# A windowed-attention stage whose values are loaded by head on partition halves, with half of the keys on ScalarE's DMA queue

## The chip, the cores and the metric

The kernel runs on one core of a Trainium2 chip. The metric is device time in microseconds (us) of one execution. The kernel before was timed in three runs: 833.41, 840.51 and 843.72 us, median 840.51 us. The changed kernel is timed in the same way. One execution of the kernel before was also recorded by the hardware profiler, and all rows of a trace below come from that one.

## What is computed

Three layers follow each other. The first is attention with eight heads over 4 sequences of 576 tokens, 64 numbers per head. Four heads see the last 32 tokens, the other four see every fourth of the last 128. The second layer sends each token to one of eight experts, the third is a dense layer.

```python
# q, k, v: (4, 8, 576, 64) float32
scores = matmul(q, k^T) / sqrt(64)
mask_plain = (rel >= 0) & (rel < 32)                    # heads 0..3
mask_dil   = (rel >= 0) & (rel < 128) & (rel % 4 == 0)  # heads 4..7
attn = softmax(where(mask, scores, -1e9));  x = matmul(attn, v)  # -> (2304, 512)
# experts: each token goes to the best of 8 by cosine similarity
out[mask] = gate_w * (relu(x[mask] @ w1[e]) @ w2[e])    # 512 -> 1024 -> 512
# dense: 512 -> 2048 -> 512
h = x @ w_in;  out = (h * cos(h)) @ w_out
```

## The kernel before

The 2304 tokens are 18 tiles of 128. Inputs come in pairs of tiles: nine pairs, each with a queries tile `q`, keys and values. Two heads share the 128 partitions, 64 each: partitions 0 to 63 hold one head (j = 0), 64 to 127 the other (j = 1), and four such head pairs (`pr`) make the eight heads.

**Keys and values.** `kr` is a ring of six tiles of keys, `[128, 2, 6, 512]`, block-diagonal: half j of the partitions holds head j's keys in plane j, and zeros in the other plane, so that one matmul over 128 partitions gives the scores of both heads side by side. `vb` is built in the same way: two buffers `[128, 2, 2, 4, 4, 65]`, one pair of tiles each, half j filled in plane j and the rest set to zero once by GpSimd (L349, L352, L368). The 65th column is one, so a product also gives the row sum. Because a half and a plane go together, keys and values are loaded by two DMAs of 64 partitions each (L333 for keys, 256 KB each; L338 for values, 520 KB each). Queries come in one DMA over 128 partitions (L330, 512 KB). All of these are issued by SyncE (SP), in program order.

**A tile.** `emit_S` (L425, L429) adds the mask by one bf16 matmul and the scores by 16 float32 matmuls of 32 columns of weights. VectorE (DVE) takes the maximum and subtracts it, ScalarE (ACT) takes the exponential (`emit_E`, L445), TensorE (PE) transposes (L452), ACT copies the transpose to `pT` (L457), and `emit_PV` (L465) multiplies it by the values: 16 matmuls over 128 partitions with 130 columns, into two PSUM banks by `pr // 2`. `emit_N` divides by the row sum. Later in the pipeline come the transposes of x (L487), the logits of the experts, and the store of x, 256 KB a tile, to the DRAM tensor `x_d`, issued by ACT (L525).

**What sets the order.** The first 15 tiles run in a hand-written loop (`TURN` = 15), whose steps stand in one string, `ORDER`, with lags of 0 to 3 tiles: scores of tile i, products of tile i - 1, logits of tile i - 3. Its step `l`, in the middle of an iteration between the copy `pT` and the exponential on ACT, is the place where the next loads are issued: in odd iterations keys and queries of pair i // 2 + 2, in even ones from 2 on the values of pair i // 2 + 1. The last three tiles, the ranking of tokens by expert and the preparation of the first expert weights (loads `wst`, 1024 KB each, L241, whose absolute sums ACT takes at L250) are ordered by a planner from due times. In its terms the values of pair p may be loaded after the products of tile 2p - 3. At 154 us SP loads the list of tokens by expert (`ix`, L856); expert matmuls begin at 171 us, the dense layer at about 450 us.

**DMA semaphores.** DMAs issued by SP and by ACT's queue take eight semaphores in turn (DMAHW0 to DMAHW7). A DMA that takes a semaphore waits at its queue until the DMA that had that semaphore before has landed.

Of the kernel before, what the change touches and what calls it, by code (L numbers as in the profile page):

```python
# [11 lines left out]
F32 = mybir.dt.float32  # L12
# [7 lines left out]
ALU = mybir.AluOpType  # L20
# [145 lines left out]
def tile_kernel(ctx, tc, qh, kh, vh, c16_h, c32_h, emb, tau, w1h, w2h, win_h, wout_h, out):  # L166
    nc = tc.nc
    V, S, G, T, SP = nc.vector, nc.scalar, nc.gpsimd, nc.tensor, nc.sync
# [59 lines left out]
    with tc.manual_schedule():  # L228
        wst = ctx.enter_context(tc.tile_pool(name="wst", bufs=5, side="left"))
        with ExitStack() as p12:  # L230
# [5 lines left out]
            plan = Plan(HOLD1, BIAS1)  # L236
# [69 lines left out]
            with ExitStack() as p1:  # L306
                krp = p1.enter_context(tc.tile_pool(name="krp", bufs=1, side="right"))
                cst = p1.enter_context(tc.tile_pool(name="p1c", bufs=1, side="right"))
# [7 lines left out]
                sm = p1.enter_context(tc.tile_pool(name="sm", bufs=3, side="right"))  # L316
                ps_s = p1.enter_context(tc.tile_pool(name="ps_s", bufs=2, space=PSUM))
                ps_1 = p1.enter_context(tc.tile_pool(name="ps_1", bufs=1, space=PSUM))
                kr = krp.tile([128, 2, RING, 512], F32, name="kr")
                krb = kr.rearrange("p j s (b i) -> p j (s b) i", i=32)  # L320
                vb = [cst.tile([128, 2, 2, 4, 4, 65], F32, name=f"vb{i}") for i in range(2)]
                blank = cst.tile([128, E * REG // 64], U32, name="blank")
                tau_b = cst.tile([128, 1], F32, name="tau_b")
                ent = cst.tile([128, 4, E], F32, name="ent")
# [2 lines left out]
                def load(p, i0=0, i1=2):  # L327
                    if i0 == 0:
                        q_t[p] = qp.tile([128, 2, 4, 128], F32, name="q", tag="q")
                    SP.dma_start(out=q_t[p][:, i0:i1], in_=qh[p, :, i0:i1])  # L330
                    s0 = (2 * p) % RING
                    for j in range(2):
                        SP.dma_start(out=kr[64 * j:64 * j + 64, j, s0 + i0:s0 + i1], in_=kh[p, 64 * j:64 * j + 64, i0:i1])  # L333

                def load_v(p, i0=0, i1=2):
                    v = vb[p % 2]
                    for j in range(2):
                        SP.dma_start(out=v[64 * j:64 * j + 64, j, i0:i1], in_=vh[p, 64 * j:64 * j + 64, i0:i1])  # L338


                zc = cst.tile([128, 1], F32, name="zc")
# [4 lines left out]
                other = lambda j: slice(64 * j, 64 * j + 64)  # L346
                for j in range(2):
                    S.activation(out=kr[other(j), 1 - j, 0], in_=zc[other(j)].to_broadcast([64, 512]), func=ACTF.Copy)
                    G.memset(vb[0][other(j), 1 - j, 0], 0.0)  # L349
                for j in range(2):  # L350
                    V.memset(kr[other(j), 1 - j, 1:RING - 1], 0.0)
                    G.memset(vb[0][other(j), 1 - j, 1], 0.0)  # L352
                c16_load = lambda a, b: SP.dma_start(out=c16[:, a:b], in_=c16_h[:, a:b])
                load(0, 0, 1)
                c16_load(0, 640)
                load(0, 1, 2)
# [7 lines left out]
                load_v(0, 1, 2)  # L364
                c16_load(1152, 3 * 128 + NT * 128)
                load_v(1)
                for j in range(2):
                    G.memset(vb[1][other(j), 1 - j], 0.0)  # L368
                G.memset(zero, 0)
                G.memset(blank, 0)  # L370
                SP.dma_start(out=tok_r.rearrange("(p a) w -> p (a w)", p=128), in_=blank)
# [9 lines left out]
                def set_up(k):  # L381
                    if k == 0:
                        V.tensor_copy(out=pay[:, :, 0], in_=tokf)
                        V.tensor_scalar(out=base, in0=iota, scalar1=float(REG), scalar2=None, op0=ALU.mult)
                        V.tensor_copy(out=base0, in_=base)
                        V.tensor_tensor(out=tri, in0=iota.unsqueeze(1).to_broadcast([128, E, E]), in1=iota.unsqueeze(2).to_broadcast([128, E, E]), op=ALU.is_lt)
                        V.tensor_tensor_reduce(out=esq, in0=emb_t, in1=emb_t, scale=1.0, scalar=0.0, op0=ALU.mult, op1=ALU.add, accum_out=ess)
                    elif k == 1:
                        G.tensor_tensor(out=ess, in0=ess, in1=half[0:E, 0:1], op=ALU.pow)
                    elif k == 2:  # L390
                        V.tensor_scalar(out=ess, in0=ess, scalar1=1e-6, scalar2=None, op0=ALU.add)
                        V.reciprocal(out=ess, in_=ess)
                        V.reciprocal(out=tau_b, in_=tau_b)
                        V.tensor_scalar(out=emb_t, in0=emb_t, scalar1=ess, scalar2=tau_b[0:E], op0=ALU.mult, op1=ALU.mult)
                    elif k == 3:
                        for c in range(4):
                            T.transpose(eps[:, c, :], emb_t[:, c * 128:(c + 1) * 128], ident[0:E, 0:E])
                    else:
                        V.tensor_copy(out=ent, in_=eps)

                st = {}
# [56 lines left out]
                    st["pT", t] = pT  # L458

                def emit_PV(t):  # L460
                    pT, v = st.pop(("pT", t)), vb[(t // 2) % 2][:, :, t % 2]
                    xps = ps_1.tile([128, 2, 512], F32, name="xps", tag="xps")
                    for pr in (2, 3, 0, 1):
                        for u in range(4):
                            T.matmul(out=xps[32 * u:32 * u + 32, pr // 2, 130 * (pr % 2):130 * (pr % 2) + 130],  # L465
                                     lhsT=pT[:, pr, 32 * u:32 * u + 32], rhs=v[:, :, u, pr, :], start=True, stop=True)
                    st["xps", t] = xps

                def emit_N(t, k):
                    xv = st["xps", t][:, :, 0:260].rearrange("p a (h c) -> p a h c", c=65)  # L470
                    if k == 0:
                        st["rs", t] = sm.tile([128, 2, 4, 1], F32, name="rs", tag="rs")
                        V.tensor_scalar(out=st["rs", t], in0=xv[:, :, :, 64:65], scalar1=1e-9, scalar2=None, op0=ALU.add)
                    elif k == 1:
                        V.reciprocal(out=st["rs", t], in_=st["rs", t])
                    elif k == 2:
                        xd = st["xd", t] = xp.tile([128, 256], F32, name="xd", tag="xd", bufs=2)
                        V.tensor_tensor(out=xd.rearrange("p (h c) -> p h c", c=64), in0=xv[:, 1, :, 0:64], in1=st["rs", t][:, 1].to_broadcast([128, 4, 64]), op=ALU.mult)
                    else:
                        x = st["x", t] = xp.tile([128, D], F32, name="x", tag="x")  # L480
                        V.tensor_tensor(out=x[:, 0:256].rearrange("p (h c) -> p h c", c=64), in0=xv[:, 0, :, 0:64], in1=st["rs", t][:, 0].to_broadcast([128, 4, 64]), op=ALU.mult)

                def emit_XT(t):
                    x, xd = st["x", t], st.pop(("xd", t))
# [145 lines left out]
                def fetch(what, p):  # L630
                    if p < NT // 2 and (what, p) not in fetched:
                        fetched.add((what, p))
                        (load if what == "k" else load_v)(p)
# [8 lines left out]
                for i in range(TURN):  # L642
                    if 0 < i < 4:
                        for k in ((0, 1), (2,), (3, 4))[i - 1]:
                            set_up(k)
                    count = {}
                    for what in ORDER.split():
                        if what == "r":
                            pump()
                        elif what == "w":  # L650
                            if i >= W_FROM:
                                take(early)
                        elif what == "L":
                            for _ in range(WLOADS.count(i)):
                                take(loads)
                        elif what == "l":
                            if i % 2 == 1:
                                fetch("k", i // 2 + 2)
                            elif i > 1:
                                fetch("v", i // 2 + 1)  # L660
                        else:
                            lag, *parts = tile_jobs[what]
                            if i >= lag:
                                parts[count.get(what, 0)](i - lag)
                            count[what] = count.get(what, 0) + 1
# [3 lines left out]
                for q in plan.free:  # L669
                    plan.free[q] = 0.0  # L670
                for p in range(2, NT // 2):
                    for what, after in (("k", "S"), ("v", "PV")):
                        if (what, p) not in fetched:
                            plan.add((what, p), "DMA", 2.9, lambda what=what, p=p: fetch(what, p), (after, 2 * p - 3))
                        else:
                            plan.at((what, p), 0.0)
                for t in range(TURN - 3, NT):
# [158 lines left out]
            with ExitStack() as p2:  # L836
# [42 lines left out]
                ixs, xrs, xps = {}, {}, {}  # L879
# [158 lines left out]
                for e in range(E):  # L1038
                    plan.add(("list", e), "DMA", 0.5, lambda e=e: x_do(e, 0, "list"), ("sent", NT - 1), *[("gate", e - 2, c) for c in range(3)])
                    for c in range(3):  # L1040
                        k = 3 * e + c
# [13 lines left out]
                    for f in range(8):  # L1055
                        pe(("mm", 2 * e, f), 1.35, lambda e=e, f=f: h_part(e, f), ("x lo", e, 0), ("x lo", e, 1), ("lo", 2 * e, f * CUT // 8), *([("h lo", (4 * e + f // 2 - 3) // 4, (4 * e + f // 2 - 3) % 4)] if f % 2 == 0 else []))
                        if f % 2:
                            k = f // 2
# [7 lines left out]
                    for i, ds in enumerate(halves):  # L1066
                        for f in range(8):
                            name = ("mm", 2 * e + 1, f) if not i else ("mm", 2 * E, f)
# [73 lines left out]
        with ExitStack() as p3:  # L1142
# [124 lines left out]
            for b, (t0, n) in enumerate(blocks):  # L1267
# [11 lines left out]
                for t in range(n // 128):  # L1279
# [11 lines left out]
                    c = t0 // 128 + t  # L1291
# [66 lines left out]
```

## Time and profile before

| what | value |
|---|---|
| median of three runs | 840.51 us |
| the profiled execution | 842.5 us |
| its span in the trace | 840.7 us |
| TensorE busy | 749.1 us, 89% of the span |
| ScalarE, VectorE, GpSimd busy | 448.9, 438.6, 188.8 us |
| mean granted TensorE clock | 0.935 of full speed |

The span runs from the first to the last instruction of the trace; the execution's own time is 1.8 us longer. TensorE is the busiest engine over the whole span, but the share is uneven: the attention stage, the first fifth of the span, is where it waits most, and it is the only stage that the change touches.

### The profile page before, as it was taken

Reading aid. Unit: us, or ns where it says so; the run is one execution under the profiler, and the core shown is the slowest. Engines: PE = TensorE matmul, PEld = TensorE weight load, DVE = VectorE, ACT = ScalarE, POOL = GpSimd, SP = SyncE. Lnnn points to the kernel's source line nnn. Section 1 sums busy time; section 2 is a strip of 40 time slices with the busy share of each in tenths; the row PEclk is TensorE's granted clock in tenths of the full one; section 3 lists DMA queues with packets and bytes.
Section 4 is the critical chain, followed back from the end, with each engine's and each line's share of the span. In section 5 each row is a group of like instructions: output and inputs, shape, how many; then the busy total and the mean of one; then the engine's idle time right before and its main releaser. Section 6 shows DMA issues by size and latency. Waiting matters only on the chain. (4 is left out here: it accounts for less than half of the span.)

```text
span 840.7 us, 14816 instructions
## 1 busy us (share of the span) xinstructions
PE 749.1 (89%) x5961; PEld 492.2 (59%) x5961; DVE 438.6 (52%) x893; ACT 448.9 (53%) x705; POOL 188.8 (22%) x230
## 2 busy tenths in 40 slices
PE   6897779494999889988997989999999999999995
PEld 3676667273898768876883434444444445645642
DVE  5354525655678587857797983154105511531510
ACT  2343536362778698857566992177117701832820
POOL 4021203375010010100000440234103411421420
PEclk8888968887899989998999999999999999999999
DMA  8979881559855566635321000100000000000000
GB/s 220 257 170 253 219 294 52 212 102 103 262 177 194 192 218 211 241 126 165 115 76 55 1 0 1 46 5 2 26 26 1 0 26 26 1 14 26 1 13 26
DMA packets 27444, 87.32 MB, mean 104 GB/s; under 512 B 9688, under 2 KB 10200, under 8 KB 22240
## 3 DMA queue, kind: packets, MB, share of 16 engines
q1 hardware_dynamic: 20256, 70.42, 28.8%
q0 software_dynamic: 4512, 11.04, 4.7%
q10 hardware_dynamic: 2592, 4.72, 1.8%
q8 instruction: 55, 0.90, 0.5%
q14 instruction: 29, 0.24, 0.1%
HBM read 76.53 MB, written 9.64 MB: 102 GB/s over the span
## 5 line engine op out<-in xcount | busy, mean ns | idle before, releaser
L1188 PE MATMUL u<-yb,win 128*128 128x512 f16 (+1 forms) x924 | 179.8, 357 | 0.0
L1226 PEld LDWEIGHTS <-g 128*128 128x128 f16 x864 | 85.0, 98 | 105.7 <-issue 4.2
L1226 PE MATMUL o<-wst,g 128*128 128x512 f16 x672 | 145.7, 379 | 0.0
L1188 PEld LDWEIGHTS <-win 128*128 128x128 f16 x924 | 90.4, 98 | 88.8
L1004 PE MATMUL hps<-xT,wt 128*128 128x256 f16 x768 | 98.2, 292 | 19.9 <-DVE xT L877 13.9
L1222 POOL TENSOR_TENSOR g<-gg,g 128x512 f16<-128x512 f32 (+1 forms) x80 | 85.4, 1071 | 125.3 <-ACT g L1220 124.2
L973 PE MATMUL y<-h,wt 128*128 128x256 f16 (+1 forms) x1152 | 107.7, 255 | 1.1 <-DVE h L963 0.3
L973 PEld LDWEIGHTS <-wt 128*128 128x128 f16 x1152 | 96.4, 98 | 11.2 <-issue 2.2
L1004 PEld LDWEIGHTS <-wt 128*128 128x128 f16 x768 | 80.3, 105 | 35.5 <-issue 19.6
L1217 DVE SCALAR_TENSOR_TENSOR gg<-u,q 128x512 f32<-128x512 f32 (+1 forms) x80 | 50.6, 637 | 73.7 <-ACT q L1214 73.5
L1209 ACT ACTIVATE kk<-u,quart,ku 128x512 int32<-128x512 f32 (+1 forms) x80 | 58.1, 732 | 51.3 <-PE u L1188 51.1
L275 DVE SCALAR_TENSOR_TENSOR wt<-wst,wsc,wt 128x1024 f16<-128x1024 f32 x64 | 79.4, 1280 | 3.8 <-ACT wt L273 2.8
L273 ACT ACTIVATE wt<-wst,wsc 128x1024 f16<-128x1024 f32 x64 | 69.0, 1142 | 12.3 <-DVE wsc L217 7.9
L250 ACT ACTIVATE junk<-wst 128x2048 bf16<-128x2048 f32 x32 | 61.0, 1906 | 24.7 <-DMA wst<-in_w1h 24.6
L861 POOL DMA_INDIRECT xr<-x_d,ix x24 | 28.0, 1166 | 203.4 <-PE hps L870 103.0
L1212 DVE SCALAR_TENSOR_TENSOR q<-u,ku,kk 128x512 f32<-128x512 f32 (+1 forms) x80 | 54.8, 689 | 32.3 <-ACT kk L1209 32.3
L1214 ACT ACTIVATE q<-q,quart 128x512 f32<-128x512 f32 (+1 forms) x80 | 53.1, 669 | 5.7 <-DVE q L1212 5.4
L1288 ACT ACTIVATE osb<-o,ku 128x512 f32<-128x512 f32 x6 | 4.1, 687 | 97.3 <-PE o L1226 97.3
L1290 DVE TENSOR_SCALAR osb<-o,ku 128x512 f32<-128x512 f32 x8 | 6.0, 751 | 92.4 <-PE o L1226 92.4
L1294 POOL DMA_INDIRECT out<-osb,idx x18 | 17.5, 971 | 150.0 <-DVE osb L1290 93.7
L1220 ACT ACTIVATE g<-gg 128x512 f16<-128x512 f32 (+1 forms) x80 | 45.8, 575 | 1.4 <-DVE gg L1217 1.4
L1226 PE MATMUL u<-wst,g 128*128 128x512 f16 x192 | 43.4, 390 | 2.7 <-ACT wst L808 2.1
(197 smaller groups left out, 889.0 us busy)
## 6 DMA issues: line engine op xcount, KB each, us to landing
wst<-in_w1h SPq DMA_DIRECT2D x16, 1024.0 KB, 6.6
wst<-in_w2h SPq DMA_DIRECT2D x16, 1024.0 KB, 5.1
vb<-in_vh SPq DMA_DIRECT2D x16, 520.0 KB, 9.4
raw<-in_winh SPq DMA_DIRECT2D x16, 512.0 KB, 7.2
raw<-in_wouth SPq DMA_DIRECT2D x16, 512.0 KB, 3.9
x_d<-x ACTq DMA_DIRECT2D x18, 256.0 KB, 5.2
q<-in_qh SPq DMA_DIRECT2D x8, 512.0 KB, 8.3
kr<-in_kh SPq DMA_DIRECT2D x16, 256.0 KB, 9.7
```

The costliest lines, as they stand in the source:

```text
L250: S.activation(out=junk[:, 0:k], in_=src, func=ACTF.Square, accum_out=wmx[m][:, i:i + 1])
L273: S.activation(out=hi, in_=src, func=ACTF.Copy, scale=wsc[:, m, 0:1])
L275: V.scalar_tensor_tensor(out=lo, in0=src, scalar=wsc[:, m, 0:1], in1=hi, op0=ALU.mult, op1=ALU.subtract)
L973: T.matmul(out=dst(d), lhsT=w[:, a, 128 * d:128 * d + 128], rhs=src(f, b), start=f == 0 and k == 0 and d in firsts, stop=f == 7 and k == 2 ...
L1004: T.matmul(out=hps[e, f // 2][:, f % 2], lhsT=w[:, a, 128 * c:128 * c + 128], rhs=xts[e][0][:, 4 * b + c, :], start=n == 0, stop=n == 11)
L1188: T.matmul(out=us[f], lhsT=win[f][:, a, 128 * c:128 * c + 128], rhs=ybs[b][:, a2, c, :], start=k == 0, stop=k == 11)
L1209: S.activation(out=ks[f], in_=us[f], func=ACTF.Identity, scale=ku[:, 0:1], bias=quart[:, 0:1])
L1212: V.scalar_tensor_tensor(out=qs[f], in0=us[f], scalar=ku[:, 0:1], in1=ks[f], op0=ALU.mult, op1=ALU.subtract)
L1214: S.activation(out=qs[f], in_=qs[f], func=ACTF.Sin, scale=PI2, bias=quart[:, 1:2])
L1217: V.scalar_tensor_tensor(out=gs[f], in0=us[f], scalar=SH, in1=qs[f], op0=ALU.mult, op1=ALU.mult)
L1222: G.tensor_tensor(out=g_t[f][:, 1], in0=gs[f], in1=g_t[f][:, 0], op=ALU.subtract)
L1226: T.matmul(out=o, lhsT=g_t[f][:, a, 128 * t:128 * t + 128], rhs=wout[f][:, a2, :], start=f == 0 and k == 0, stop=f == 15 and k == 2)
```

## The change

Values. `vb` becomes three buffers `[128, 2, 4, 4, 65]` without the second plane: half j of the partitions holds head j's values and there are no zeros. One DMA over 128 partitions loads a pair (1040 KB), and GpSimd's memsets are gone. In the loop the values are fetched one pair earlier; in the planner they wait for the products of tile 2p - 5.

Products. Each of the 16 matmuls over 128 partitions and 130 columns becomes two, one for each head, over 64 partitions and 65 columns. The two write to different PSUM banks (j instead of `pr // 2`). `emit_N` reads the same number of elements in another arrangement.

Keys. The half j = 0 stays on SP's queue, the half j = 1 is issued by ACT.

```diff
-                vb = [cst.tile([128, 2, 2, 4, 4, 65], F32, name=f"vb{i}") for i in range(2)]
+                vb = [cst.tile([128, 2, 4, 4, 65], F32, name=f"vb{i}") for i in range(3)]
+                head = lambda j: slice(64 * j, 64 * j + 64)
-                    for j in range(2):
-                        SP.dma_start(out=kr[64 * j:64 * j + 64, j, s0 + i0:s0 + i1], in_=kh[p, 64 * j:64 * j + 64, i0:i1])
+                    for j, queue in enumerate((SP, S)):
+                        queue.dma_start(out=kr[64 * j:64 * j + 64, j, s0 + i0:s0 + i1], in_=kh[p, 64 * j:64 * j + 64, i0:i1])
                 def load_v(p, i0=0, i1=2):
-                    v = vb[p % 2]
-                    for j in range(2):
-                        SP.dma_start(out=v[64 * j:64 * j + 64, j, i0:i1], in_=vh[p, 64 * j:64 * j + 64, i0:i1])
+                    SP.dma_start(out=vb[p % 3][:, i0:i1], in_=vh[p, :, i0:i1])
-                    G.memset(vb[0][other(j), 1 - j, 0], 0.0)
-                    G.memset(vb[0][other(j), 1 - j, 1], 0.0)
-                for j in range(2):
-                    G.memset(vb[1][other(j), 1 - j], 0.0)
                 def emit_PV(t):
-                            T.matmul(out=xps[32 * u:32 * u + 32, pr // 2, 130 * (pr % 2):130 * (pr % 2) + 130],
-                                     lhsT=pT[:, pr, 32 * u:32 * u + 32], rhs=v[:, :, u, pr, :], start=True, stop=True)
+                            for j in range(2):
+                                T.matmul(out=xps[32 * u:32 * u + 32, j, 65 * pr:65 * pr + 65], lhsT=pT[head(j), pr, 32 * u:32 * u + 32],
+                                         rhs=v[head(j), u, pr, :], start=True, stop=True)
                 def emit_N(t, k):
-                    xv = st["xps", t][:, :, 0:260].rearrange("p a (h c) -> p a h c", c=65)
+                    xv = st["xps", t][:, :, 0:260].rearrange("p j (r c) -> p r j c", c=65)
-                            elif i > 1:
-                                fetch("v", i // 2 + 1)
+                            else:
+                                fetch("v", i // 2 + 2)
-                    for what, after in (("k", "S"), ("v", "PV")):
+                    for what, after in (("k", ("S", 2 * p - 3)), ("v", ("PV", 2 * p - 5))):
```

On SP's queue, from the values of pair 1 on, the program of before reads as follows (`vb_131` and `vb_132` are the two buffers, `x2` the two halves).

```order
L338 DMA vb_132<-in_vh 64x2080 x2
L371 DMA tok_r<-blank 128x336
L330 DMA q<-in_qh 128x1024
L333 DMA kr<-in_kh 64x1024 x2
L338 DMA vb_131<-in_vh 64x2080 x2
L330 DMA q<-in_qh 128x1024
L333 DMA kr<-in_kh 64x1024 x2
```

In the changed kernel the same place of SP's queue reads as below, with a third buffer `vb_133`.

```order
L338 DMA vb_132<-in_vh 128x2080
L367 DMA tok_r<-blank 128x336
L338 DMA vb_133<-in_vh 128x2080
L332 DMA q<-in_qh 128x1024
L335 DMA kr<-in_kh 64x1024
L338 DMA vb_131<-in_vh 128x2080
L332 DMA q<-in_qh 128x1024
L335 DMA kr<-in_kh 64x1024
```

The values of pair 2 now stand ahead of the queries and keys of pair 2, and so on for each pair: values are one pair ahead, and a pair takes three DMAs of SP's queue instead of five.

ACT's program in the changed kernel starts as follows, up to iteration 3 of the loop (`DMAHW` names the DMA semaphore that a transfer waits for, `zc` is a column of zeros); in the kernel before the rows at L335 are not there.

```order
L348 ACT_TABLE_LOAD
L348 ACTIVATE kr<-zc 64x512 [waits DVE_49]
L348 ACTIVATE kr<-zc 64x512
L335 DMA kr<-in_kh 64x512 x2
L335 DMA kr<-in_kh 64x1024 [waits DMAHW1_49]
L441 ACTIVATE pt<-sb 128x512 [waits DVE_49]
L453 ACTIVATE pT<-ptp 128x512 [waits PE_49]
L335 DMA kr<-in_kh 64x1024 [waits DMAHW6_49]
...
L453 ACTIVATE pT<-ptp 128x512 [waits PE_49,Activation_49]
L335 DMA kr<-in_kh 64x1024 [waits DMAHW5_49,DMAHW4_49]
L441 ACTIVATE pt<-sb 128x512 [waits DVE_49]
```

ACT issues three halves before its first exponential, and from then on one in each odd iteration, between a copy `pT` and the next exponential. The semaphores that these rows wait for were taken by transfers issued two or three iterations earlier.

On PE a stretch of the loop's start reads as follows in the changed kernel. In the kernel before it is the same, but the row of the products is `xps<-vb_131,pT 32x130 x16`.

```order
L421 LDWEIGHTS c_111
L421 MATMUL s<-c_111 128x512
L425 MATMUL s<-kr,q 32x128 x16
L448 MATMUL ptp<-c_63,pt 128x128 x4
L462 MATMUL xps<-vb_131,pT 32x65 x32
```

There are twice as many products with half the columns each; the order of PE's work around them has not moved.

## Rows read from the trace of the kernel before

**Rows 1.** The page: span, and TensorE and DMA busy tenths in 40 slices.
```profile
span 840.7 us, 14816 instructions
...
PE   6897779494999889988997989999999999999995
...
DMA  8979881559855566635321000100000000000000
```

**Rows 2.** Windows: stretch and length, busy us by engine, granted clock, DMA share, GB/s.
```profile
28.00:32.00 4.00, 2.48 (x45) 1.99 (x43) 1.67 (x4) 1.42 (x4) 0.00 (x0) 1.00 1.02 228
63.00:66.00 3.00, 3.00 (x58) 2.46 (x50) 2.20 (x11) 1.13 (x3) 0.00 (x0) 1.00 0.93 374
112.00:118.00 6.00, 3.40 (x58) 2.55 (x60) 1.49 (x6) 3.61 (x6) 0.00 (x0) 0.78 1.01 418
```

**Rows 3.** DMA issues on the page: count, KB each, median us to landing.
```profile
vb<-in_vh SPq DMA_DIRECT2D x16, 520.0 KB, 9.4
x_d<-x ACTq DMA_DIRECT2D x18, 256.0 KB, 5.2
q<-in_qh SPq DMA_DIRECT2D x8, 512.0 KB, 8.3
kr<-in_kh SPq DMA_DIRECT2D x16, 256.0 KB, 9.7
```

**Rows 4.** Windows of the attention stage, columns as in rows 2.
```profile
0.00:100.00 100.00, 82.30 (x1236) 61.16 (x1240) 50.51 (x172) 40.12 (x86) 22.59 (x35) 0.86 0.89 220
0.00:114.40 114.40, 90.34 (x1365) 67.58 (x1365) 55.76 (x192) 43.51 (x93) 22.59 (x35) 0.85 0.90 232
116.50:133.50 17.00, 16.57 (x151) 14.50 (x155) 5.28 (x26) 9.94 (x19) 4.24 (x7) 0.50 0.43 168
```

**Rows 5.** PE's timeline: start us, us, engine, line, [idle before, releaser].
```profile
17.26 0.58 PE L425 MATMUL s<-c 128*128 128x512 bf16 x1 [3.90 <-DMA c<-in_c]
...
51.45 0.38 PE L425 MATMUL s<-c 128*128 128x512 bf16 x1
...
54.43 1.09 PE L465 MATMUL xps<-vb,pT 128*32 128x130 f32 x32
...
55.95 0.38 PE L425 MATMUL s<-c 128*128 128x512 bf16 x1
...
71.18 1.10 PE L429 MATMUL s<-kr,q 128*32 128x128 f32 x32 [4.27 <-DMA kr<-in_kh]
...
99.75 1.08 PE L429 MATMUL s<-kr,q 128*32 128x128 f32 x32
...
107.45 1.94 PE L429 MATMUL s<-kr,q 128*32 128x128 f32 x32 [6.29 <-DMA kr<-in_kh]
...
170.92 0.37 PE L1004 MATMUL hps<-xT,wt 128*128 128x256 f16 x1 [0.47 <-ACT xT L875]
```

**Rows 6.** Waits of SP's DMA queue, 0 to 160 us: us in total, times, longest.
```profile
SPq L333 <- DMA x_d<-x: 23.3, 4, 9.6
SPq L338 <- DMA x_d<-x: 11.0, 2, 10.4
SPq L338 <- PE xps L465: 10.8, 3, 6.5
SPq L241 <- DMA x_d<-x: 8.9, 2, 4.5
```

**Rows 7.** ACT's timeline: the first activations, and a wait for weights.
```profile
2.02 1.26 ACT L348 ACTIVATE kr<-zc 64x512 f32<-64x512 f32 x2
...
114.39 1.91 ACT L250 ACTIVATE junk<-wst 128x2048 bf16<-128x2048 f32 x1 [10.58 <-DMA wst<-in_w1h]
```

**Rows 8.** SP's timeline: the first keys, and the list of tokens by expert.
```profile
1.19 1.19 SPq L333 DMA_DIRECT2D kr<-in_kh  x2
...
154.22 0.38 SPq L856 DMA_DIRECT2D ix<-tok_r  x1
```

**Rows 9.** Groups by shape, 0 to 130 us: GpSimd's memset of a buffer of values.
```profile
L368 POOL MEMSET vb<- 64x2080 f32 x2 | 3.7, 1828 | 0.1
```

**Rows 10.** Windows of the expert stage and of the dense stage, columns as in rows 2.
```profile
170.00:450.00 280.00, 242.81 (x2436) 213.22 (x2435) 202.95 (x345) 197.07 (x270) 42.40 (x53) 0.93 0.56 166
450.00:800.00 350.00, 346.01 (x1690) 165.96 (x1689) 145.25 (x231) 174.35 (x288) 98.62 (x106) 0.99 0.03 12
```

More of the change, by code (lines that the diff above doesn't have):

```diff
@@ L460, in emit_PV @@
                 def emit_PV(t):
-                    pT, v = st.pop(("pT", t)), vb[(t // 2) % 2][:, :, t % 2]
+                    pT, v = st.pop(("pT", t)), vb[(t // 2) % 3][:, t % 2]
                     xps = ps_1.tile([128, 2, 512], F32, name="xps", tag="xps")
@@ L464, in emit_PV @@
                         for u in range(4):
-                            T.matmul(out=xps[32 * u:32 * u + 32, pr // 2, 130 * (pr % 2):130 * (pr % 2) + 130],
-                                     lhsT=pT[:, pr, 32 * u:32 * u + 32], rhs=v[:, :, u, pr, :], start=True, stop=True)
+                            for j in range(2):
+                                T.matmul(out=xps[32 * u:32 * u + 32, j, 65 * pr:65 * pr + 65], lhsT=pT[head(j), pr, 32 * u:32 * u + 32],
+                                         rhs=v[head(j), u, pr, :], start=True, stop=True)
                     st["xps", t] = xps
                 def emit_N(t, k):
-                    xv = st["xps", t][:, :, 0:260].rearrange("p a (h c) -> p a h c", c=65)
+                    xv = st["xps", t][:, :, 0:260].rearrange("p j (r c) -> p r j c", c=65)
                     if k == 0:
-                        st["rs", t] = sm.tile([128, 2, 4, 1], F32, name="rs", tag="rs")
+                        st["rs", t] = sm.tile([128, 4, 2, 1], F32, name="rs", tag="rs")
                         V.tensor_scalar(out=st["rs", t], in0=xv[:, :, :, 64:65], scalar1=1e-9, scalar2=None, op0=ALU.add)
@@ L477, in emit_N @@
                         xd = st["xd", t] = xp.tile([128, 256], F32, name="xd", tag="xd", bufs=2)
-                        V.tensor_tensor(out=xd.rearrange("p (h c) -> p h c", c=64), in0=xv[:, 1, :, 0:64], in1=st["rs", t][:, 1].to_broadcast([128, 4, 64]), op=ALU.mult)
+                        V.tensor_tensor(out=xd.rearrange("p (r j c) -> p r j c", r=2, j=2), in0=xv[:, 2:4, :, 0:64], in1=st["rs", t][:, 2:4].to_broadcast([128, 2, 2, 64]), op=ALU.mult)
                     else:
                         x = st["x", t] = xp.tile([128, D], F32, name="x", tag="x")
-                        V.tensor_tensor(out=x[:, 0:256].rearrange("p (h c) -> p h c", c=64), in0=xv[:, 0, :, 0:64], in1=st["rs", t][:, 0].to_broadcast([128, 4, 64]), op=ALU.mult)
+                        V.tensor_tensor(out=x[:, 0:256].rearrange("p (r j c) -> p r j c", r=2, j=2), in0=xv[:, 0:2, :, 0:64], in1=st["rs", t][:, 0:2].to_broadcast([128, 2, 2, 64]), op=ALU.mult)
                 def emit_XT(t):
@@ L671, in tile_kernel @@
                 for p in range(2, NT // 2):
-                    for what, after in (("k", "S"), ("v", "PV")):
+                    for what, after in (("k", ("S", 2 * p - 3)), ("v", ("PV", 2 * p - 5))):
                         if (what, p) not in fetched:
-                            plan.add((what, p), "DMA", 2.9, lambda what=what, p=p: fetch(what, p), (after, 2 * p - 3))
+                            plan.add((what, p), "DMA", 2.9, lambda what=what, p=p: fetch(what, p), after)
                         else:
```

## The prediction

> **What bounds the kernel now.** I read the page first: TensorE (PE) is at nine tenths or more from the 25th of the 40 slices to the last but one, and lowest in the first eight, of which the first six (21 us each) have the DMA engines at seven tenths or more [rows 1]. The change touches only these first 154 us. The later stages take over whatever is gained there: in the dense stage PE is busy 346.0 of 350 us, and in the expert stage 242.8 of 280 us with DMA at 0.56, so neither waits for transfers that an earlier start would make later [rows 10]. A microsecond gained when expert matmuls begin (170.92 us [rows 5]) is a microsecond at the end.
>
> In the attention stage the reader should see two near-equal limits. PE alone needs 4.50 us a tile at full clock: the mask matmuls of two tiles start at 51.45 and 55.95 us with no stall between [rows 5]. Yet from the masks at 17.26 us (tile 2) to the scores at 99.75 us (tile 15) 13 tiles take 82.5 us, 6.3 each. The long stalls of PE name keys: 4.27 us at 71.18, 6.29 us at 107.45 [rows 5]. The DMA engines are busy 0.89 of the first 100 us, at only 220 GB/s [rows 4]. Two things waste them. Transfers to 64 partitions are slow: with values and keys alone in flight the engines are full at 228 GB/s, against 374 with queries and weights and 418 with weights [rows 2]. And SP's queue stands still: 23.3 us in four waits of keys for a store of x, 11.0 us in values for the same, 10.8 us in values for products that still read the buffer [rows 6].
>
> **The change part by part.**
>
> *Values in one load.* A pair of tiles is 2 x 520 KB [rows 3], 1.065 MB. At 228 GB/s it takes 4.67 us of the DMA engines, at 380 (between 374 and 418) 2.80 us: 1.87 us less per pair. By 99.75 us eight pairs were loaded (15.0 us of DMA time), by 114.4 us all nine (16.8 us). The bounds are nothing (other queues already fill the gaps beside half loads) and these figures; I take the whole, because rows 2 shows a full share at 228 GB/s, so nothing fills the gaps there.
>
> *Third buffer, values a pair earlier.* The wait for products (10.8 us [rows 6]) goes from SP's queue. The values of pair 2 now stand ahead of the keys of pair 2, 2.8 us of transfer; those keys are wanted at tile 4. Since c16's masks hold PE until 17.26 us (3.90 us idle [rows 5]) and fewer microseconds of values (about 1) lie ahead of them, I let tile 2 start 2 us earlier, at 15.3, and tile 4 is then due near 25, when pair 2's keys should have landed. If not, PE waits 1 to 3 us there once.
>
> *Half the keys on ACT.* It adds 11 DMA issues to ACT's queue and takes them from SP's. An issue by SP is about 0.6 us (two in 1.19 us [rows 8]), and ACT is busy 40.1 of the first 100 us [rows 4]; 0.6 us in every second tile is hidden there. At the start the zeros in `kr` keep ACT until 3.28 us [rows 7], while SP issued both halves from 1.19 us [rows 8]: first scores are up to 2 us later, but the masks of tile 2 have a later release, so I cost it at nothing (if uncovered: 2 us). I credit no bandwidth: the keys are still two transfers on 64 partitions. What this edit does give is that SP passes one semaphore less per pair, so it meets fewer fresh stores of x: the 34.3 us of store waits in keys and values should mostly go.
> The Trainium skill, "SBUF — State Buffer", section "Can I just issue two DMAs to hit both halves?", says that two transfers on the two halves run after each other, from several engines too, and gained 6% together. By that rule the keys gain nothing either; no run here shows it yet.
>
> *Products per head.* 32 products over half the columns. Nothing in the trace has this shape. The nearest row is today's: 32 records (16 float32 products in two passes) in 1.09 us [rows 5], bound by 130 columns for four column groups at once. Below: half the columns with all eight groups at once, 0.55 us a tile. Above: 64 passes at today's 34 ns each, 2.18 us. Between lies the same 1.09 us (heads not overlapping). I take 0.8, nearer to the lower since columns, not count, set today's row: 0.3 less a tile, 4 us over 13 tiles of PE time. The masks' spacing then becomes 4.2, with ranking work in some iterations about 4.6.
>
> *GpSimd's memsets* (two of 1.83 us [rows 9], and smaller) were beside other work: nothing.
>
> *The sum.* By PE, tile 15 comes at 15.3 + 13 x 4.6 = 75 us. By DMA: 0.89 x 100 = 89 us busy, less 15.0, is 74 us; the queue that no longer waits might reach a share of 0.95, so 78 + 1 us before the first transfer = 79. Two limits so near each other don't mesh perfectly; I take 80, a gain of 20. Next is ACT's wait of 10.58 us for weights that ended at 114.39 us [rows 7], with the DMA engines full until then [rows 2]: busy 0.90 x 114.4 = 103 us, less 16.8, is 86; at 0.95 it is 91, plus 1 is 92. Gain 22. From there to the list at 154.22 us [rows 8] the planner's order is unchanged. Of it 17 us ran at a granted clock of 0.50 with PE busy 16.57 [rows 4], 8 us more than at full clock; it followed PE's stalls at 107.45 and behind ACT's wait. Shorter stalls may keep half of it: 4 us. Together 26 us, so the list comes near 128 us, expert matmuls near 145, and the profiled execution at 842.5 - 26 = 816.5 us. The profiled execution of before is 2.0 us above the median of the three (840.51), so against the median the forecast is 814.5. If half-clock stretches and the meshing go well (gain 36) it is 804.5, if the share stays at 0.89 and the clock is not better (gain 16), 824.5: this is the forecast's own range.
>
> **The rivals.**
>
> *Values gain only the waits.* Half loads may share the engines with queries and stores, so that the isolated 228 GB/s is not what they cost. Then full share moves what the mean rows say: 220 / 0.89 = 247 GB/s, 22.0 MB by tile 15 in 89 us, tile 15 at 90, the weights at 103: gain 11, with 2 of clock 13, and 827.5. For it speaks that windows with values in them mix many transfers; against it the full share at 228.
>
> *Products cost by number.* At 34 ns a pass, 2.18 us: 1.09 more a tile instead of 0.3 less, 1.39 x 13 = 18 us over the PE limit of 75. Tile 15 comes at 93, and the last three tiles add 4 in the planned part: gain of 20 falls to 7, less 4, plus the clock: about 5 to 8, 834. Against it: today's records come in groups of four, which count alone would not make.
> The Trainium skill, "TensorE: Matmul & The Clock Gate", section "Wait — 56ns, not 53.3ns?", says that starts are never under about 25 ns apart, however small the matmul; by this, an estimate, 64 passes take 1.6 us. Whether that holds across array parts the traces here don't show, and it would be 822.
>
> *ACT's queue stands still* (the other side). A key transfer on ACT that must wait for its semaphore stops the exponential behind it, then the transposes and products, and with them PE. Its price is a landing: keys take 9.7 us in the median [rows 3], and the waits of SP for stores up to 9.6 [rows 6]. Seven odd iterations of the loop could be hit. It cancels the 26 us at 3.7 us of net delay each, and gives slower by over 2% at (26 + 17) / 7 = 6.1; at the full 9.6 less 1.5 us of slack the time is 814.5 + 57 = 871. Against it: the transfers waited for were issued two or three iterations (9 to 14 us) earlier, longer than the 9.7.
>
> *Given back later.* The list comes earlier but the first expert's weights do not: their transfers go past the list, and expert matmuls begin at 165 instead of 145. Gain 6: 834.5. Against it: the wait that ends at 114.39 us [rows 7] is for such weights, 40 us ahead of the list; they come with the gain, not behind it.
>
> **How the numbers follow.** Chances: the forecast 0.66, values gain only the waits 0.14, products by number 0.07, ACT's queue 0.07, given back later 0.06. The prediction is 814.5 us. The range 800 to 832 takes in the forecast's own range (804.5 to 824.5), a little beyond it, and the first rival; it leaves out the other three. Two per cent, about what a measurement of this kernel can tell from no change, is 17 us: faster is below 823.7, slower above 857.3. Faster: nearly all of the forecast and some of the first rival, 0.67. Slower: ACT's queue only, 0.06. The rest, 0.27, is the same.
>
> **What would show it.** Values: landing times of one 1040 KB load under 3 us where nothing else flies, and over 330 GB/s at full share. Queue: no waits of SP's keys for stores of 5 us and more. Products: L462 at 0.5 to 0.9 us a tile. PE: tile 15's scores near 80 us and no wait of several us for keys. ACT: no idle time at L441 behind an issue at L335. Passing on: expert matmuls near 145 us, and from there to the end as long as before (840.7 - 170.9 = 669.8 us). The prediction is wrong if tile 15 is later than 90 us, if ACT waits at L335, or if that last stretch grows.

## The result and the profile after

The changed kernel takes 833.11 us (median of 12 runs, 824.06 to 841.53) against 842.63 us (median of 12 runs) before. The ratio is 0.9872, with a 95% interval of 0.9828 to 0.9916. It is taken from the runs within 1.5% of the fastest of each kernel, so it is a little lower than that of the medians. The kernel is faster, by 1.3% and not by the 3.1% that was forecast: less than the 2% that the prediction asked of "faster". The median lies just outside the range of 800 to 832 us.

The profiled execution of the changed kernel takes 827.0 us. On its page, TensorE's (PE) and the DMA engines' busy tenths look much as in [rows 1].

```profile
span 825.2 us, 15933 instructions
...
PE   6879889358999889969888989999999999999995
...
DMA  8996930876656467543330000100000000000000
```

The windows of the attention stage (columns as in [rows 2]) answer to [rows 4] in their first line. The second runs from the mask of tile 2 to that of tile 15, the third is a long stretch at half clock.

```profile
0.00:100.00 100.00, 77.93 (x1804) 58.59 (x1804) 53.09 (x183) 43.69 (x93) 15.17 (x29) 0.93 0.87 262
14.53:95.59 81.06, 66.13 (x1530) 51.78 (x1531) 39.65 (x144) 35.52 (x79) 13.56 (x22) 0.92 0.88 258
106.80:130.60 23.80, 23.54 (x247) 20.45 (x247) 10.38 (x61) 16.06 (x28) 8.11 (x13) 0.50 0.18 65
```

The DMA engines move 262 GB/s instead of 220 at the same share, so the loads are better. But PE is busy 77.9 us of the first 100 instead of 82.3. Part of that is work that takes less time, since the granted clock is 0.93 and not 0.86; the rest is that PE waits less for loads and more for something else. PE's timeline (start, length, engine, line, records, idle time before and its releaser) shows where; lines 421, 425 and 462 answer to 425, 429 and 465 in [rows 5].

```profile
14.53 0.55 PE L421 MATMUL s<-c 128*128 128x512 bf16 x1 [1.94 <-DMA c<-in_c]
...
28.67 1.93 PE L425 MATMUL s<-kr,q 128*32 128x128 f32 x32 [1.79 <-DMA kr<-in_kh]
...
38.02 0.86 PE L462 MATMUL xps<-vb,pT 64*32 64x65 f32 x64
...
46.18 1.08 PE L425 MATMUL s<-kr,q 128*32 128x128 f32 x31 [1.17 <-issue]
...
52.86 0.85 PE L425 MATMUL s<-kr,q 128*32 128x128 f32 x20 [0.88 <-issue]
...
57.73 0.64 PE L425 MATMUL s<-kr,q 128*32 128x128 f32 x14
60.99 0.82 PE L425 MATMUL s<-kr,q 128*32 128x128 f32 x18 [2.62 <-issue]
...
66.84 1.94 PE L425 MATMUL s<-kr,q 128*32 128x128 f32 x32
...
95.59 0.38 PE L421 MATMUL s<-c 128*128 128x512 bf16 x1
```

The mask of tile 2 comes 2.7 us earlier than before (the forecast had 2). From there to the mask of tile 15 it takes 81.1 us for 13 tiles (82.2 before), so the tile pace has hardly moved. Tile 15 itself is later than 90 us, which the prediction had named as a sign that it is wrong. The stalls of 4 and 6 us for keys are gone, and so is ACT's wait of 10.58 us for weights [rows 7]. In their place PE stops in the middle of a group: after the 14th of 32 records of one tile's scores it stands still for 2.62 us, and nothing in the profile released it ("issue"). At 66.84 the next scores take 1.94 us instead of 1.08: the granted clock is at its lower level (0.51 from 62.2 to 68.6 us).

SP's waits, 0 to 160 us, answer to [rows 6]: of the waits for stores of x none of note is left. SP now waits for PE, that is, for buffers, and for key transfers to land (9.0 us here, 8.1 and 6.7 us at other lines).

```profile
SPq L338 <- PE xps L462: 30.2, 5, 8.0
SPq L338 <- DMA kr<-in_kh: 9.0, 1, 9.0
SPq L332 <- PE s L425: 8.5, 4, 5.2
```

The list of tokens is loaded at 144.73 us (154.22 before [rows 8]) and expert matmuls begin at 160.99 (170.92 before [rows 5]).

```profile
144.73 0.39 SPq L854 DMA_DIRECT2D ix<-tok_r  x1
...
160.99 0.37 PE L1002 MATMUL hps<-xT,wt 128*128 128x256 f16 x1 [0.47 <-ACT xT L873]
```

What stands still is seen in the DMA view of three short windows ahead of such stalls: 43.7 to 44.1, 50.4 to 50.8 and 58.3 to 58.7 us, stalls ending at 46.18, 52.86 and 60.99. Each has one packet of the instruction queue (q8: packets, MB, share of the engines).

```profile
q8 instruction: 1, 0.02, 17.0%
```

```profile
q8 instruction: 1, 0.02, 14.5%
```

```profile
q8 instruction: 1, 0.02, 18.6%
```

Each of the three stalls ends 2.5 to 2.7 us after the start of its window. The others are no different: all nine stalls with no releaser between 14 and 106 us end 2.3 to 2.8 us after a packet of the instruction queue started. The reading is that PE has run out of instructions and waits for the next block, which travels on the same DMA engines as the data. The experiments test the number of instructions.

### The profile page after: what moved, and what is told of

It is laid out like the page before. It is cut to its first block, busy times and chain, and to the rows that moved or that the text cites. A ratio compares the mean times of both kernels' runs of the same rounds, so it can differ in the third digit from the quotient of the medians.

```text
span 825.2 us, 15933 instructions
## 1 busy us (share of the span) xinstructions
PE 736.4 (89%) x6537; PEld 484.2 (59%) x6537; DVE 436.4 (53%) x893; ACT 448.9 (54%) x705; POOL 180.5 (22%) x224
## 5 line engine op out<-in xcount | busy, mean ns | idle before, releaser
L971 PE MATMUL y<-h,wt 128*128 128x256 f16 (+1 forms) x1152 | 109.7, 257 | 11.1 <-issue 10.1
L1002 PE MATMUL hps<-xT,wt 128*128 128x256 f16 x768 | 94.3, 284 | 17.7 <-DVE xT L875 10.6
```

Source lines behind the costliest of these rows:

```text
L971: T.matmul(out=dst(d), lhsT=w[:, a, 128 * d:128 * d + 128], rhs=src(f, b), start=f == 0 and k == 0 and d in firsts, stop=f == 7 and k == 2 ...
L1002: T.matmul(out=hps[e, f // 2][:, f % 2], lhsT=w[:, a, 128 * c:128 * c + 128], rhs=xts[e][0][:, 4 * b + c, :], start=n == 0, stop=n == 11)
```

## The experiments

Two theories stood against each other for the missing 15 us (26 forecast, 10.8 by the ratio). **Instructions**: with 32 products a tile instead of 16, PE needs its instructions faster than they come and stops for them. **Loads**: the one load for two heads, or the keys on ACT's queue, brings less than the rows promised.

### Taking the parts apart

Only the values and products, with both key halves on SP:

```diff
-                    for j, queue in enumerate((SP, S)):
-                        queue.dma_start(out=kr[64 * j:64 * j + 64, j, ...
+                    for j in range(2):
+                        SP.dma_start(out=kr[64 * j:64 * j + 64, j, ...
```

> The changed kernel with both key halves back on SP's queue: only the values and the products are changed. If ACT's key transfers cost or give nothing, the time is that of the changed kernel (about 0.987 of before, tile 17's mask near 101 us, the list near 145 us). If they were what took SP past the stores of x, SP waits for stores again by 10 us and more, the keys come late, and the time goes back towards before (above 0.995). If they hold ACT up, this kernel is faster than the changed one (below 0.98).

Measured: 824.44 us, 0.9865 of before (0.9813 to 0.9916). That is the changed kernel's ratio. In its profile the list comes at 135.00 us, 10 us earlier than the expectation's 145, though the time is the same. SP's waits for stores of x, 43.2 us in [rows 6], are 4.1 us here, with both halves on SP: it was not the keys on ACT that took them away.

Only the key halves, the same edit the other way round in the kernel before:

> The kernel before with only the key halves split between SP's and ACT's queues. If the two halves on two queues bring nothing, it takes 0.995 to 1.005 of before, with PE still stalled by several us for keys at tiles 10 and 17. If the gain of the change came from here, it takes about 0.987, the stalls for keys shrink below 2 us.

Measured: 837.83 us, 1.0017 of before (0.9984 to 1.0049). The keys' place gives nothing and costs nothing that can be measured, alone or together with the rest. The stalls for keys that the expectation had staying did shrink (none over 0.9 us), and the time did not follow. In this profile SP waits 20.0 us for stores of x instead of 46.1, but 32.3 us instead of 2.5 for key transfers to land.

Only the depth: the kernel before, with a third block-diagonal buffer and values a pair earlier.

```diff
-  vb = [cst.tile([128, 2, 2, 4, 4, 65], F32, name=f"vb{i}") for i in range(2)]
+  vb = [cst.tile([128, 2, 2, 4, 4, 65], F32, name=f"vb{i}") for i in range(3)]
-  elif i > 1:
-      fetch("v", i // 2 + 1)
+  else:
+      fetch("v", i // 2 + 2)
```

> The kernel before, block-diagonal values in two loads, with a third buffer and values fetched a pair earlier (a scratch tile that nobody reads has one buffer instead of two to make room). If depth is what gains, the time is below 0.99 of before and the list near 140 us. If the rate of the loads is what gains, it is 0.995 to 1.005 and the list within 5 us of 154.

Measured: 837.41 us, 0.9947 (0.9909 to 0.9986), the list at 148.34 us. Depth alone is worth half a per cent, and the list is 5.9 us earlier: between the two outcomes of the expectation. With slow loads the keys still come late, as PE's timeline of this kernel shows.

```profile
36.10 1.93 PE L431 MATMUL s<-kr,q 128*32 128x128 f32 x32 [6.79 <-DMA kr<-in_kh]
```

### The number of products, at the same work

The kernel before, with each product of 130 columns cut into two of 65:

```diff
-  T.matmul(out=xps[..., pr // 2, 130 * (pr % 2):130 * (pr % 2) + 130],
-           lhsT=pT[:, pr, 32 * u:32 * u + 32], rhs=v[:, :, u, pr, :], ...)
+  for j in range(2):
+      T.matmul(out=xps[..., pr // 2, 130 * (pr % 2) + 65 * j:130 * (pr % 2) + 65 * j + 65],
+               lhsT=pT[:, pr, 32 * u:32 * u + 32], rhs=v[:, j, u, pr, :], ...)
```

> The kernel before with each product of 130 columns cut into two of 65, over all 128 partitions, in the same bank: 32 products a tile, the same columns. If PE's instruction supply stalls it when a tile has more instructions, PE's idle time put down to issue grows from about 3 us by 4 us or more between tiles 2 and 15 and the time is 0.5 to 1.5% above before. If only columns count, the products take 1.1 us a tile as before and the time is that of before within 0.3%. If their number counts, the products take about 2.2 us a tile and the time rises by some 10 us.

Measured: 846.08 us, 1.0131 of before (1.0073 to 1.0190): 11 us more, for the same columns. The products themselves cost hardly more. In the groups by shape, 0 to 130 us (records, busy us, mean ns, idle before and its releasers), the first line is of before, the second of this kernel.

```profile
L465 PE MATMUL xps<-vb,pT 128*32 128x130 f32 x544 | 23.8, 322 | 6.8 <-issue 2.6 <-ACT pT L457 2.6 <-DMA vb<-in_vh 1.6
```

```profile
L466 PE MATMUL xps<-vb,pT 128*32 128x65 f32 x1088 | 24.7, 245 | 12.9 <-issue 6.8 <-ACT pT L457 5.9 <-DMA vb<-in_vh 0.2
```

Busy time goes from 23.8 to 24.7 us; the idle time in front of the products doubles, and half of it has no releaser. PE's waits from 14 to 97 us (us in total, times, longest) name issue first:

```profile
PE s L429 <- issue: 4.7, 3, 3.1
PE xps L466 <- issue: 3.8, 3, 2.2
```

The longest stalls (3.09 and 2.93 us) end at 66.49 and 102.46 us in the middle of a group, like those of the changed kernel. In the DMA view of 63.9 to 64.3 us there is again one packet of the instruction queue. The profiled execution was the shortest of the four (839.15 us), and its list, at 153.74 us, is level with that of before: the price stands in the times, and this one profile shows only the stalls.

Then the loads without the number. This kernel has the changed loads and 16 products over both heads at once, so that two heads are added up; tokens go to other experts, and everything behind the list differs from before. Its time says nothing beside before; its attention stage does, and it is the base for the next run.

```diff
-  for j in range(2):
-      T.matmul(out=xps[..., j, 65 * pr:65 * pr + 65], lhsT=pT[head(j), pr, ...], rhs=v[head(j), u, pr, :], ...)
+  h = pr - pr % 2
+  T.matmul(out=xps[..., pr // 2, 130 * (pr % 2):130 * (pr % 2) + 130], lhsT=pT[:, pr, ...], rhs=v[:, u, h:h + 2, :], ...)
```

> The changed kernel with 16 products of 128 partitions and 130 columns as before, so that the two heads are added up (the attention output is not computed rightly; work per engine is as before). If the number of PE's instructions is what eats the gain of the loads, issue stalls fall from about 7 to 3 us between tiles 2 and 15, tile 15 comes 4 us or more earlier than 95.6 us, and the list before 140 us. If the number doesn't matter, tile 15 and the list stay within 2 us of the changed kernel, or come later by the products' longer time (0.2 us a tile).

Measured: 925.86 us; the mask of tile 15 at 88.14 us, the list at 127.44 us. The list is where the forecast had put it (128), by another way: the sum had tile 15 at 80 us and 6 us gained behind it, here they are 88.1 and 15.5. PE's waits from 14 to 97 us have almost no issue left; the first lines are loads.

```profile
PE s L425 <- DMA kr<-in_kh: 3.5, 2, 2.7
PE s L421 <- DMA c<-in_c: 2.4, 1, 2.4
...
PE lgx L495 <- issue: 0.5, 1, 0.5
```

The same kernel with each product cut in two, 65 columns and 128 partitions, in the same bank:

> The kernel with the changed loads and 16 products of 130 columns (which adds up two heads, so that routing and the later stages differ from before; it is to be compared with that kernel alone, 925.9 us or 1.106 of before), with each product cut into two of 65 columns in the same bank: only the number of PE's instructions differs. If instruction supply is what eats the gain, PE's idle time with no releaser between tiles 2 and 15 goes from 0.6 to 6 us or more, the list from 127.4 us to 134 or later, and the time rises by about 10 us (ratio 1.115 or more). If it was something of the two-head form (64 partitions, two banks), the time stays within 3 us.

Measured: 938.71 us, 12.9 us more than with 16 products (925.86), at the same routing. The two were timed at different times, and the kernel before, timed beside each, took 835.29 and 839.96 us. By the ratios to it, 1.1060 (1.1004 to 1.1116) and 1.1159 (1.1097 to 1.1221), the price is about 8 us. In the profiles the list comes at 140.33 us, 12.9 us later, so the difference is made in the attention stage. PE's waits, 14 to 97 us:

```profile
PE xps L463 <- ACT pT L453: 4.8, 4, 2.1
PE s L421 <- DMA c<-in_c: 3.6, 1, 3.6
...
PE s L425 <- issue: 2.4, 2, 2.0
...
PE xps L463 <- issue: 1.0, 1, 1.0
```

Of the list's 12.9 us the stalls themselves are 2.7 us (3.4 against 0.7; the expectation had 6 us or more), the waits for `pT` 4.1 more (4.8 against 0.7). Before the list, PE is busy 17.7 us at a granted clock of 0.50 against 10.0, which costs at most half of the difference, 3.9 us, as an estimate. That the two-head form (64 partitions, two banks) costs something of its own is not borne out: here it is absent, and the number still has a price of this size.

The changed kernel once more, for a second profile:

> The changed kernel once more, for a second profile and more times. If PE's stalls for instructions belong to it and not to one execution, idle time with no releaser between tiles 2 and 15 is 5 us or more again, tile 15's mask comes at 92 to 99 us, the list at 135 to 146, and the time is 0.983 to 0.992 of before.

Measured: 825.74 us, 0.9872 (0.9799 to 0.9944). The mask of tile 15 at 91.20 (0.8 us earlier than expected), the list at 138.76, expert matmuls at 155.42 us; PE's issue stalls from 14 to 97 us are 6.8 us again (7.1 in the first profile between the masks of tiles 2 and 15, 4.4 before).

One execution scatters, though: the kernel with only the keys moved, which has 16 products, shows 6.8 us of issue as well, in four stalls. But only one of these, 2.98 us, ends within 2.1 to 3.0 us of the start of an instruction packet; of the four before it is one too, 1.89 us. Counting only such stalls, 14 to 97 us, the nine traces with 16 products have 0 to 3.0 us and the five with 32 have 3.5 to 7.3. So stalls behind an instruction packet go with the number of products in every trace here; the price of the number in time rests on the two timed pairs (11 and 8 us by the ratios).

The place of the list in one execution scatters as well: 144.73 and 138.76 us for the changed kernel, 135.00 with both key halves on SP. Spells at half the granted clock account for much of it. Before the list, PE is busy at 0.50 for 36.9, 41.9 and 19.3 us in these three, 45.4 us in the kernel before and 10.0 us with 16 products.

### Two buffers, and three attempts at keeping 16 products

The kernel of 16 products with two buffers and the old order of loads:

> The same kernel of 16 products with two buffers of values and the old order of loads: the values in one load alone. If the faster load is what gains, the list stays below 133 us (127.4 with three buffers). If the third buffer and the earlier place are what gains, SP waits for products again by 8 us or more and the list goes back to 145 us or later (154.2 before).

Measured, one run: the list at 146.98 us, and SP's waits for products from 0 to 125 us are these (columns as above).

```profile
SPq L338 <- PE xps L462: 49.5, 7, 10.0
```

With three buffers they are 21.1 us and the list 127.44. So the one load needs the third buffer: at the list, depth alone gave 5.9 us, the load alone (154.22 to 146.98) 7.2, both together 26.8. These are single executions, and the place of the list scatters by up to 10 us.

Next, right results with 16 products: one load into a staging buffer, and GpSimd copies each half into a block-diagonal buffer.

```diff
+  def spread(t):
+      p, i = t // 2, t % 2
+      for j in range(2):
+          G.tensor_copy(out=vb[p % 2][64 * j:64 * j + 64, j, i], in_=vstg[p % 2][64 * j:64 * j + 64, i])
```

> Values of pair 1 on in one load into a staging buffer, and GpSimd copies each half into block-diagonal buffers, so that there are 16 products a tile and the result is right. If the loads gain 27 us at the list when PE has 16 products, and GpSimd's copies (1 to 2 us each, four a pair) are hidden, the list comes at 128 to 135 us and the time is 0.965 to 0.98 of before, below the changed kernel. If copies hold up PE or the port that GpSimd and VectorE use, PE waits for vb and the time is no better than 0.987.

Measured: 823.93 us, 0.9818 (0.9752 to 0.9884), the list at 136.99 us: a little behind the first outcome of the expectation. Its ratio is the lowest of this study, but its interval overlaps that of the changed kernel. The copies take 1.05 us each, and GpSimd's scatters of the list stand in their way:

```profile
L347 POOL COPY vb<-stg 64x1040 f32<-64x1040 f32 x32 | 33.6, 1051 | 32.0 <-DMA tok_r<-pay,slot_u 16.3 <-DMA stg<-in_vh 13.3 <-PE lgx L508 1.1
```

The copies one tile earlier in GpSimd's program (`spread(i + 2)` for `spread(i + 1)`), without and with half of the keys on ACT:

> GpSimd's spreading of the values one tile earlier, so that a wait of GpSimd's scatter of the list (about 6 us each) is covered. If those waits kept the values late, SP's waits for GpSimd's copies fall from 14.7 to below 5 us, the list comes near 130 us and the time is 0.970 to 0.980 of before. If the loads or PE's own work bound it, it stays at 0.982.

> The same with half of the keys on ACT's queue. If the place of the keys' issue gives nothing, as alone, it is within 0.3% of the kernel without it; if it takes SP past the stores of x here, where SP has more loads to place ahead, it is 0.3 to 0.8% faster.

Measured: 1.0036 (0.9999 to 1.0072) and 1.0045 (1.0014 to 1.0076). Neither outcome of the first expectation came. Earlier copies lose everything: PE waits 8.1 us for them, as the groups by shape of the first show, and why the copies come so late was not followed up. The keys' place again makes no difference.

```profile
L473 PE MATMUL xps<-vb,pT 128*32 128x130 f32 x544 | 21.2, 301 | 9.8 <-POOL vb L347 8.1 <-DMA vb<-in_vh 1.7
```

Copies shared between GpSimd and VectorE:

> As the first kernel with GpSimd spreading the values, but from tile 4 on VectorE copies the second half, so that a tile's values are ready after one copy of each engine. If GpSimd's copies (33.6 us of it, behind the scatters) kept values and loads late, SP's waits for GpSimd's copies fall from 14.7 to some 5 us, the list comes near 130 us and the time is 0.970 to 0.978 of before. If VectorE's added copies (about 0.6 to 1.1 us a tile) delay the softmax, PE's idle time for DVE and ACT grows and the time is at or above the 0.982 of that kernel.

Measured: 1.0124 (1.0083 to 1.0166). VectorE's copy was written behind the load that fills the staging buffer again, so it waits for that load and takes values of a later pair. The run therefore leaves its question open.

## Why the prediction was wrong, point by point

- **Values in one load, a pair earlier**: right in mechanism. The loads bring 262 GB/s instead of 220 over the first 100 us, and per busy time of the engines 262 / 0.87 = 301 GB/s instead of 247, about what the sum needs (22.0 MB in 74 us). That puts out the rival "values gain only the waits", which kept 247. That the list comes at 127.4 us with 16 products, where the sum had 128, is partly luck. PE is busy 10.0 us at half clock before it instead of 45.4, worth up to 18 us as an estimate, where the sum had 4 us for the clock, and tile 15 is 8 us later than in the sum. The wait of 1 to 3 us for the keys of pair 2 came too (1.79 us at 28.67). What the text had not seen is that load and third buffer need each other.
- **Half the keys on ACT**: right that it brings no bandwidth and that ACT doesn't stand still (no wait of note before its exponentials behind an issue, so the slower rival is out). ACT gets 10 issues, not 11. The credit for SP's waits for stores went to the wrong part: they are gone with both halves on SP as well, and the keys' place alone gives 1.0017.
- **Products per head**: here the step failed. The length was well estimated (0.8 us a tile; 0.86 at full clock, 1.09 before [rows 5]). But the text took the shorter length as 4 us off PE's floor and priced the doubled number of instructions at nothing. By the ratios the number costs 11 us (6 to 16) in the kernel before and about 8 us with the changed loads. Forecast 26 us, less 8 to 11, leaves 15 to 18; measured are 10.8 by the ratio. The other 4 to 7 us are open; the half clock below is one candidate.
- **The rival "products by number"** had the outcome (834 us) with a chance of 0.07, but by another mechanism: 34 ns for each pass, 2.18 us a tile. That is out, and so is the estimate of 1.6 us: a tile's 64 passes take 0.86 us, 13 ns each. The cost lies in stalls in whatever group PE reaches when its instructions run out, scores as well as products.
- **PE's floor of 4.6 us a tile** was near: from the mask at 35.05 to that at 40.15 and 44.41 us, tiles take 5.1 and 4.3 us. But the sum took 13 tiles at the floor, while the trace of before has stalls with no releaser that the prediction's list of long stalls left out. The second, 1.89 us in mid-group, ends 2.7 us after an instruction packet started, and could have warned that PE's supply is near its limit; the first, 1.52 us, has no packet in the 11 us before its end.

```profile
29.84 1.08 PE L429 MATMUL s<-kr,q 128*32 128x128 f32 x32 [1.52 <-issue]
...
35.26 1.02 PE L465 MATMUL xps<-vb,pT 128*32 128x130 f32 x10 [1.89 <-issue]
```

- **Half clock**: 4 us back were counted on behind tile 17. The first profile has the reverse, 23.8 us at 0.50 (17.0 before [rows 4]); the second profile isn't better (0.50 from about 102 to 122 us). In both it follows a stall behind an instruction packet, of 2.73 us up to 105.46 and 2.47 us up to 101.15.
- **Passed on**: right. From the first expert matmul to the end it is 664.2 us (825.2 - 161.0), against 669.8 before; in the second profile 668.4.
- **A small misreading**: TensorE is lowest in the eighth slice and in the tenth alike (4 tenths [rows 1]), not in the first eight alone. Nothing in the sum rests on it.

The instruction supply as the cause is a reading of the rows: stalls in mid-group with no releaser, a packet of the instruction queue some 2.5 us ahead of the end of all nine in the changed kernel's profile, and a price that follows the number of instructions at equal columns. What the experiments show is the price of the number; the way in between was not taken away by itself. Packets alone don't make stalls: the kernel with the changed loads and 16 products has 11 of them from 14 to 97 us, as many as the kernel before with 32, and 0.7 us of stalls. The Trainium skill, "Runtime: NRT & Kernel Launch", section "Instruction fetch mechanics", says that instructions arrive by DMA in blocks of 16 KiB and that crossing into the next block is mostly hidden. The packets of 0.02 MB agree with the first; the stalls of 0.9 to 2.6 us looked at above do not agree with the second, in a stage whose DMA engines are 0.88 busy.

## What to carry to other kernels

Where matmuls are small and the DMA engines nearly full, as here, count PE's instructions as a resource of their own: halving the columns of a product saved 0.23 us a tile, some 4 us over 18 tiles, and doubling their number cost 8 to 11 us. Look in the trace of before for stalls with no releaser, and whether a packet of the instruction queue started some 2.5 us ahead of their end; here that told such stalls from others. To price a restructuring, cut the present matmuls in two without changing anything else: that one kernel gives the cost of the number, and would have given it here ahead of the change (11 us, with an interval of 6 to 16).

## What was not expected of the hardware

Twice as many matmuls over the same columns left PE's busy time nearly as it was (23.8 and 24.7 us) and yet cost 11 us. And a single stall of some 2 to 3 us could be followed by a spell at half the granted clock: after the 2.62 us at 60.99 the scores at 66.84 took 1.94 instead of 1.08 us, so that this stall cost more than its own length. It is not so each time: after the wait of 2.09 us that ended at 87.56, the next scores took 1.08 us.
